# Two dense products of a float32 retention block by one level of Strassen

## The chip, the core and the metric

The kernel runs on one core of one Trainium2 chip. The metric is the device time in microseconds (us) of one execution. A profiled execution leaves a trace of every instruction; TensorE (PE) does matmuls, VectorE (DVE) and ScalarE (ACT) elementwise work, GpSimd (POOL) a little of it, and SyncE (SP) issues transfers. Weight loads of TensorE are listed as an engine of their own, PEld.

## What is computed

Two blocks in a row. The first is a recurrent retention layer (4 batches, 8 heads, 768 steps, head dimension 64), with a decay for each head:

```python
for t in range(S):
    state = gamma[None, :, None, None] * state + np.einsum('bhd,bhe->bhde', k[:, :, t], v[:, :, t])
    y[:, :, t] = scale * np.einsum('bhd,bhde->bhe', q[:, :, t], state)
```

Its result, laid out as x of 3072 tokens by 512, goes through two dense products with a leaky ReLU between:

```python
h = x @ w_in                      # 3072x512 @ 512x2048
g = np.maximum(0.01 * h, h)
return (g @ w_out).astype(np.float32)   # 3072x2048 @ 2048x512
```

Everything is computed in float32. The two weight matrices arrive as float64 and are rounded to float32 on the chip.

## The kernel before, in words

The 768 steps are cut into 6 chunks (`NC`) of 128 steps (`C`). A chunk has the same 128 steps of all 4 batches, so 512 tokens (`N`).

**Attention** of one batch of one chunk has three steps. `decay_v` lets POOL scale v by the decays (L86). `stage_a` makes the scores of the 8 heads on TensorE, even heads in one PSUM tile and odd heads in another (L97), and VectorE masks them (L102). `stage_y` multiplies the state by q (L116) and v by the masked scores (L121) into one PSUM tile `yp`; VectorE scales it into the token block `xt` (L124); then k times v (`sp`, L130) updates the state on VectorE (L134, L135). The score tiles, `yp` and `sp` share the PSUM tag `att` of 4 banks. The q/k and k/v data of a batch come in two transfers of 512 KB each on SP's queue (L80, L81), into three buffers, so three batches ahead.

**Weights** come in 32 pieces of 128 by 512 float64: 16 of `w_in`, then 16 of `w_out`. `round_words` turns a piece into float32 with five VectorE operations (L164, L169, L171, L173, L175) and two on ScalarE between the first and the fourth (L166, L167). Each rounding issues the load of the piece four further on. It all happens in the attention of chunk 0 (two pieces a batch) and in the dense products of chunk 0.

**Dense products.** `unit_h` makes 128 of the 2048 hidden features for the 512 tokens: 4 matmuls with the weights stationary and 512 token columns moving (L183), then ScalarE applies Prelu out of PSUM into `gt[f]` (L185). 16 such units make a chunk's hidden layer. `unit_o` makes the output of one batch with the hidden tokens stationary and 512 columns of `w_out` moving: 16 matmuls in four parts (L194); ScalarE copies the result (L198) and issues its store (L199).

**Order.** The order on every engine is written by hand: each engine runs its instructions in program order. The start runs the attention of chunk 0; then chunk by chunk 16 units of `unit_h` and 16 parts of `unit_o`, and in the gaps of these 32 steps the attention of the next chunk (`decay_v` at step 0 of 7 of a batch, `stage_a` at 1, `stage_y` at 4).

Of the kernel before, what the change touches and what calls it, by code (L numbers as in the profile page):

```python
# [20 lines left out]
def kernel(  # L21
# [22 lines left out]


    nc = tc.nc
    NC = S // C
    DM = H * D
    HP = H // 2
    KIN = DM // 128  # L50
    KOUT = DF // 128
    N = B * C
# [4 lines left out]
    work = ctx.enter_context(tc.tile_pool(name="work", bufs=2))  # L57
    psum = ctx.enter_context(
# [3 lines left out]
    dec = const.tile([128, HP * C + H + HP], FP32, name="dec")  # L62
    win = [[const.tile([128, W], FP32, name=f"win{r}_{i}") for i in range(KIN)]
           for r in range(DF // W)]
    wout = [const.tile([128, DM], FP32, name=f"wout{f}") for f in range(KOUT)]
    gt = [const.tile([128, N], FP32, name=f"gt{f}") for f in range(KOUT)]

# [6 lines left out]

    heads = {}

    def load(c, b):
        x = work.tile([128, 2, HP, C], FP32, tag="qk", bufs=3, name=f"qk_{c}_{b}")
        y = work.tile([128, 2, H, D], FP32, tag="kv", bufs=3, name=f"kv_{c}_{b}")
# [11 lines left out]
    def stage_a(c, b):  # L91
        x = heads[c, b][0]
        ps = [psum.tile([128, HP, C], FP32, tag="att", bufs=4, name=f"a{j}p_{c}_{b}")
              for j in range(2)]
        for a in range(HP):
            for j in range(2):
                nc.tensor.matmul(ps[j][:, a, :], lhsT=x[ts(j, 64), 1, a, :],  # L97
                                 rhs=x[ts(j, 64), 0, a, :])
        am = []
        for j in range(2):  # L100
            t = work.tile([128, HP, C], FP32, tag=f"am{j}", name=f"am{j}_{c}_{b}")
            nc.vector.tensor_tensor(out=t, in0=ps[j],  # L102
                                    in1=mask.unsqueeze(1).to_broadcast([128, HP, C]),
                                    op=ALU.mult)
            am.append(t)
        scores[c, b] = am

    def stage_y(c, b, xt):
        x, y = heads.pop((c, b))
        ks, vs = y[:, 0], y[:, 1]  # L110
        am = scores.pop((c, b))
        yp = psum.tile([128, HP, C], FP32, tag="att", bufs=4, name=f"yp_{c}_{b}")
        if c > 0:
            for a in range(HP):
                for j in range(2):
                    nc.tensor.matmul(yp[ts(j, 64), a, :], lhsT=st[b][ts(j, 64), a, :],  # L116
                                     rhs=x[ts(j, 64), 0, a, :], start=(a == 0), stop=False,
                                     skip_group_check=True)
        for a in range(HP):
            for j in range(2):  # L120
                nc.tensor.matmul(yp[ts(j, 64), a, :], lhsT=vs[:, 2 * a + j, :],  # L121
                                 rhs=am[j][:, a, :], start=(c == 0 and a == 0), stop=True,
                                 skip_group_check=True)
        nc.vector.tensor_tensor(out=xt[:, :, ts(b, C)], in0=yp, in1=gq, op=ALU.mult)  # L124
        if c == NC - 1:
            return
        sp = psum.tile([128, HP, D], FP32, tag="att", bufs=4, name=f"sp_{c}_{b}")
        for a in range(HP):
            for j in range(2):
                nc.tensor.matmul(sp[ts(j, 64), a, :], lhsT=ks[:, 2 * a + j, :],  # L130
                                 rhs=vs[:, 2 * a + j, :], start=(a == 0), stop=True,
                                 skip_group_check=True)
        if c > 0:
            nc.vector.tensor_tensor(out=st[b], in0=st[b], in1=sp, op=ALU.add)  # L134
        nc.vector.tensor_tensor(out=st[b], in0=st[b] if c > 0 else sp,  # L135
                                in1=gc.unsqueeze(2).to_broadcast([128, HP, D]), op=ALU.mult)


    pieces = [win[r][i] for r in range(DF // W) for i in range(KIN)] + wout
    first_out = KIN * (DF // W)  # L140
    raws = {}
    LOW, HIGH = 896 << 20, 1151 << 20

    def load_piece(n):
        if not f64:
            nc.sync.dma_start(out=pieces[n], in_=weights[n])
            return
        raws[n] = work.tile([128, W], I64, tag="raw", bufs=4, name=f"raw{n}")
        nc.sync.dma_start(out=raws[n], in_=weights[n])

    def round_piece(n):
        if f64:
            round_words(n)
        if n + 4 < len(pieces):
            load_piece(n + 4)

    def round_words(n):
        words = raws.pop(n).bitcast(U32).rearrange("p (n two) -> p n two", two=2)
        lo, hi = words[:, :, 0], words[:, :, 1]
        e = work.tile([128, W], U32, tag="e", name=f"e{n}")  # L160
        m = work.tile([128, W], U32, tag="m", name=f"m{n}")
        f = work.tile([128, W], FP32, tag="f", name=f"f{n}")

        nc.vector.tensor_scalar(out=e, in0=hi, scalar1=0x7FF00000, scalar2=None,  # L164
# [9 lines left out]
                                       op0=ALU.bitwise_and, op1=ALU.bitwise_or)  # L174
        nc.vector.scalar_tensor_tensor(out=pieces[n], in0=f, scalar=2.0 ** -20,  # L175
                                       in1=e.bitcast(FP32), op0=ALU.mult, op1=ALU.mult)


    def unit_h(c, f, xt):
        r, o = divmod(f * 128, W)  # L180
        hp = psum.tile([128, N], FP32, tag="h", name=f"hp_{c}_{f}")
        for i in range(KIN):
            nc.tensor.matmul(hp, lhsT=win[r][i][:, ds(o, 128)], rhs=xt[:, i, :],  # L183
                             start=(i == 0), stop=(i == KIN - 1))
        nc.scalar.activation(gt[f], hp, AF.Prelu, alpha=0.01)  # L185

    sums = {}

    def unit_o(c, b, part):
        if part == 0:  # L190
            sums[0] = psum.tile([128, DM], FP32, tag="o", name=f"op_{c}_{b}")
        op = sums[0]
        for f in range(4 * part, 4 * part + 4):
            nc.tensor.matmul(op, lhsT=gt[f][:, ts(b, C)], rhs=wout[f],  # L194
                             start=(f == 0), stop=(f == KOUT - 1))
        if part == KOUT // 4 - 1:
            ob = work.tile([128, DM], FP32, tag="ob", name=f"ob_{c}_{b}")
            nc.scalar.copy(out=ob, in_=op)  # L198
            nc.scalar.dma_start(out=out[ds(b * S + c * C, C), :], in_=ob)  # L199


    def new_xt(c):
        return work.tile([128, KIN, N], FP32, tag="xt", name=f"xt_{c}")

    def load_ahead(c, b):
        n = c * B + b + 3
        if n < NC * B:
            load(*divmod(n, B))

# [5 lines left out]
    load_piece(2)  # L215
    load_piece(3)
    load(0, 2)
# [4 lines left out]
    done = 0  # L222
    x = new_xt(0)
    for b in range(B):
        decay_v(0, b)
        stage_a(0, b)
        round_piece(done)
        round_piece(done + 1)
        done += 2
        stage_y(0, b, x)  # L230
        load_ahead(0, b)

    for c in range(NC):
        more = c + 1 < NC
        nx = new_xt(c + 1) if more else None
        for u in range(KOUT + 4 * B):
            if u < KOUT:
                unit_h(c, u, x)
            else:

                while done < min(len(pieces), first_out + 4 * (u - KOUT + 1)):
                    round_piece(done)
                    done += 1
                unit_o(c, *divmod(u - KOUT, KOUT // 4))
            if c == 0 and u < KOUT:
                round_piece(done)
                done += 1
            b, s = divmod(u, 7)
            if more and b < B:
                if s == 0:  # L250
                    decay_v(c + 1, b)
                elif s == 1:
                    stage_a(c + 1, b)
                elif s == 4:
                    stage_y(c + 1, b, nx)
                    load_ahead(c + 1, b)
        x = nx

# [19 lines left out]
def _layout(q, k, v, w_in, w_out):  # L278
# [10 lines left out]
    def tokens_first(x):  # L289
# [4 lines left out]
    DM, DF = w_in.shape  # L294
    w = np.concatenate([
        w_in.reshape(DM // 128, 128, DF // W, W).transpose(2, 0, 1, 3).reshape(-1, 128, W),
        w_out.reshape(DF // 128, 128, DM)])
    if w.dtype == np.float64:
# [28 lines left out]
```

## Time and profile before

| | us |
|---|---|
| median of 3 runs | 810.38 (809.5 to 811.61) |
| the profiled execution | 809.44 |
| its span, first to last instruction | 807.5 |

The page of the profile lists the busy time of each engine, the span in 40 slices, the chain of work that ended last, and groups of instructions by line. A row of a group reads: line, engine, operation, output<-input, partitions x elements, count | busy us, mean ns of one | idle time of the engine just before them, and who ended most of it. A row of the timeline reads: start in us, length in us, engine, line, operation, tiles, count. A float32 matmul leaves two records of matmul and two of weight load. The lengths of pipelined matmuls overlap, so a pitch is taken from start to start. Two facts to begin with: TensorE is busy for 768.1 us of the span, VectorE for 153.8, and most of VectorE's time is spent before 150 us, with the weights.

### The profile page before, as it was taken

What the parts mean: (1) busy time and instruction counts of PE and PEld (TensorE: products, weight loads), DVE (VectorE), ACT (ScalarE), POOL (GpSimd) and SP (SyncE); (2) the same over time, 40 slices, a digit from 0 to 9 for tenths busy, and PEclk for the clock granted to TensorE, in tenths of its full rate; (3) what the DMA queues carried; (4) which work ended last, traced back from release to release, by engine and by line L of the source; (5) the groups of instructions that cost most, each with busy time, mean ns of one, the idle gap of its engine ahead of it and who ended that gap; (6) DMA issues with size and microseconds to landing.
All of it is one profiled execution on the core that took longest, in us unless ns stands there. A gap on an engine that the chain in (4) does not pass through costs nothing.

```text
span 807.5 us, 6705 instructions
## 1 busy us (share of the span) xinstructions
PE 768.1 (95%) x2944; PEld 371.5 (46%) x2944; DVE 153.8 (19%) x269; ACT 111.4 (14%) x185; POOL 27.1 (3%) x29
## 2 busy tenths in 40 slices
PE   5489985999999999999999999999999999999998
PEld 4445432444454454545454444544444444444443
DVE  6968786100010010101010010100000000000000
ACT  2334342000111000111000111000111000111000
POOL 1100000000000000000000000000000000000000
PEclk8589996899999999999999999999999999999999
DMA  9645443020101210101201011102010000000000
GB/s 357 253 141 191 166 156 104 14 78 14 52 19 34 65 66 27 52 1 53 65 27 53 13 53 53 51 28 66 13 53 0 1 20 20 13 1 0 13 14 26
DMA packets 15148, 48.93 MB, mean 61 GB/s; under 512 B 1680, under 2 KB 1680, under 8 KB 15120
## 3 DMA queue, kind: packets, MB, share of 16 engines
q1 hardware_dynamic: 11664, 42.22, 15.3%
q10 hardware_dynamic: 3456, 6.29, 2.1%
q8 instruction: 23, 0.38, 0.2%
q14 instruction: 5, 0.04, 0.0%
HBM read 42.21 MB, written 6.29 MB: 60 GB/s over the span
## 4 chain that ended last, share of the span: by engine, by line
PE 90%; DVE 6%; ACT 2%; DMA 1%; issue 0%; SPq 0%
PE hp L183 42%; PE op L194 40%; PE yp L116 3%; PE yp L121 3%; PE a0p L97 2%; DVE e L173 1%; ACT e L167 1%; ACT e L166 1%; PE sp L130 1%; DVE wout L175 1%; DMA raw<-in_weights_dram 1%; DVE e L164 1%; DVE win L175 1%; DVE am L102 1%; DVE f L171 1%; DVE xt L124 0%
## 5 line engine op out<-in xcount | busy, mean ns | idle before, releaser
L194 PE MATMUL op<-wout,gt 128*128 128x512 f32 x768 | 342.9, 604 | 13.4 <-DVE wout L175 13.4
L183 PE MATMUL hp<-xt,win 128*128 128x512 f32 x768 | 337.8, 597 | 4.5 <-DVE xt L124 4.5
L194 PEld LDWEIGHTS op<-wout,gt 128*128 128x128 f32 x768 | 145.6, 192 | 195.4 <-issue 177.0
L183 PEld LDWEIGHTS hp<-xt,win 128*128 128x128 f32 x768 | 144.9, 191 | 181.5 <-issue 175.1
L185 ACT ACTIVATE gt<-hp 128x512 f32<-128x512 f32 x96 | 57.3, 597 | 298.2 <-PE hp L183 298.2
L102 DVE TENSOR_TENSOR am<-a0p,mask 128x512 f32<-128x512 f32 x24 | 16.5, 689 | 300.2 <-PE a1p L97 300.2
L198 ACT COPY ob<-op 128x512 f32<-128x512 f32 x24 | 14.0, 585 | 342.5 <-PE op L194 342.5
L124 DVE TENSOR_TENSOR xt<-yp,dec 128x512 f32<-128x512 f32 x24 | 16.6, 690 | 196.5 <-PE yp L121 196.5
L86 POOL TENSOR_TENSOR kv<-kv,dec 128x512 f32<-128x512 f32 x24 | 26.6, 1108 | 568.1 <-DMA kv<-in_kv_dram 563.0
L121 PE MATMUL yp<-am,kv 128*64 128x128 f32 x384 | 31.6, 304 | 13.7 <-issue 12.5
L97 PEld LDWEIGHTS a0p<-qk 64*128 64x128 f32 x192 | 25.4, 203 | 19.8 <-issue 14.6
L97 PE MATMUL a0p<-qk 64*128 64x128 f32 x192 | 30.2, 302 | 4.3 <-DMA qk<-in_qk_dram 4.3
L121 PEld LDWEIGHTS yp<-am,kv 128*64 128x64 f32 x384 | 24.4, 150 | 19.0 <-issue 16.5
L97 PE MATMUL a1p<-qk 64*128 64x128 f32 x192 | 30.2, 302 | 0.0
L166 ACT ACTIVATE e<-e 128x512 uint32<-128x512 uint32 x32 | 20.1, 627 | 50.6 <-DVE e L164 50.5
L173 DVE SCALAR_TENSOR_TENSOR e<-raw,e 128x512 uint32<-128x512 uint32 x32 | 22.6, 705 | 19.6 <-ACT e L167 19.6
L97 PEld LDWEIGHTS a1p<-qk 64*128 64x128 f32 x192 | 25.4, 203 | 0.0
L116 PEld LDWEIGHTS yp<-qk,st 64*64 64x64 f32 x320 | 17.7, 137 | 15.9 <-issue 15.2
L171 DVE SCALAR_TENSOR_TENSOR f<-raw,m 128x512 f32<-128x512 uint32 x32 | 23.8, 743 | 1.1
L116 PE MATMUL yp<-qk,st 64*64 64x128 f32 x320 | 22.6, 282 | 0.0
L167 ACT ACTIVATE e<-e 128x512 uint32<-128x512 uint32 x32 | 20.2, 630 | 1.0
L102 DVE TENSOR_TENSOR am<-a1p,mask 128x512 f32<-128x512 f32 x24 | 16.3, 681 | 0.0
(16 smaller groups left out, 101.5 us busy)
## 6 DMA issues: line engine op xcount, KB each, us to landing
raw<-in_weights_dram SPq DMA_DIRECT2D x32, 512.0 KB, 3.4
qk<-in_qk_dram SPq DMA_DIRECT2D x24, 512.0 KB, 3.4
kv<-in_kv_dram SPq DMA_DIRECT2D x24, 512.0 KB, 4.4
out_dram<-ob ACTq DMA_DIRECT2D x24, 256.0 KB, 2.0
dec<-decay_dram SPq DMA_DIRECT2D x1, 262.0 KB, 4.6
```

The lines of the kernel that those rows point to most:

```text
L86: nc.gpsimd.tensor_tensor(out=v, in0=v, in1=gk.unsqueeze(2).to_broadcast([128, H, D]), op=ALU.mult)
L97: nc.tensor.matmul(ps[j][:, a, :], lhsT=x[ts(j, 64), 1, a, :], rhs=x[ts(j, 64), 0, a, :])
L102: nc.vector.tensor_tensor(out=t, in0=ps[j], in1=mask.unsqueeze(1).to_broadcast([128, HP, C]), op=ALU.mult)
L116: nc.tensor.matmul(yp[ts(j, 64), a, :], lhsT=st[b][ts(j, 64), a, :], rhs=x[ts(j, 64), 0, a, :], start=(a == 0), stop=False, skip_group_che ...
L121: nc.tensor.matmul(yp[ts(j, 64), a, :], lhsT=vs[:, 2 * a + j, :], rhs=am[j][:, a, :], start=(c == 0 and a == 0), stop=True, skip_group_che ...
L166: nc.scalar.activation(e, e, AF.Relu, scale=-1.0, bias=float(HIGH))
L167: nc.scalar.activation(e, e, AF.Relu, scale=-8.0, bias=8.0 * (HIGH - LOW))
L171: nc.vector.scalar_tensor_tensor(out=f, in0=lo, scalar=2.0 ** -32, in1=m, op0=ALU.mult, op1=ALU.add)
L173: nc.vector.scalar_tensor_tensor(out=e, in0=hi, scalar=0x80000000, in1=e, op0=ALU.bitwise_and, op1=ALU.bitwise_or)
L183: nc.tensor.matmul(hp, lhsT=win[r][i][:, ds(o, 128)], rhs=xt[:, i, :], start=(i == 0), stop=(i == KIN - 1))
L185: nc.scalar.activation(gt[f], hp, AF.Prelu, alpha=0.01)
L194: nc.tensor.matmul(op, lhsT=gt[f][:, ts(b, C)], rhs=wout[f], start=(f == 0), stop=(f == KOUT - 1))
```

## The change

Both dense products are made by one level of Strassen's scheme in the form with few additions: a product of matrices cut into 2 by 2 blocks takes 7 block products instead of 8, and sums of blocks before and after.

- **Blocks.** A chunk's 512 tokens become two halves of 256 (two batches each), the 512 input dimensions two halves of 256, and the hidden features are taken in 4 units of 512, two halves of 256 each. The token block `x` holds four blocks of 256 tokens by 256 dimensions; `t` holds three differences of them. VectorE makes these with four operations a chunk (`differences`), the fourth in place.
- **Weights.** `win[u]` and `wout[u]` hold, for each of 4 units, four blocks and three sums; `sums` makes the sums with four VectorE operations once a unit is rounded. The pieces come in the order win 0, 1, wout 0, 1, win 2, 3, wout 2, 3.
- **Products.** `seven` runs the products M1, M6, M5, M4, M2, M7, M3, weights stationary, 256 token columns moving. A unit of the hidden layer has 4 matmuls a product, a half of the output (`output`, two units at once) 8. Four PSUM banks (A to D) serve the seven: M2 is added onto M1 in bank A, M7 onto M6 in B, M3 onto M5 in C. M1 and M6, M5 are read out of their bank before.
- **After the products.** `hidden` makes five additions on VectorE, two copies and four Prelu on ScalarE, and the four differences of its result for the second product. `output` does likewise; its first half leaves sums in `o`, the second adds to them and stores the four blocks, on SP's queue.
- **PSUM and SBUF.** The dense products have 6 banks, the attention tag `att` 2 instead of 4. q/k and k/v have two buffers for three, the raw weights three for four, the rest of the work tiles mostly one.
- **Order.** In the start one piece a batch is rounded; in chunk 0 four pieces in each hidden unit; after the first two hidden units the whole attention of chunk 1 with four pieces; eight pieces in the first output half. In later chunks the attention of one batch of the next chunk stands in each hidden unit.
- The output leaves in another layout and is transposed on the host.

The core of the diff:

```diff
-        ps = [psum.tile([128, HP, C], FP32, tag="att", bufs=4, name=f"a{j}p_{c}_{b}")
+        ps = [psum.tile([128, HP, C], FP32, tag="att", bufs=2, name=f"a{j}p_{c}_{b}")
...
+    units = [win[0], win[1], wout[0], wout[1], win[2], win[3], wout[2], wout[3]]
+    pieces = [w[:, 2 * h : 2 * h + 2, i, :] for w in units for h in range(2) for i in range(2)]
...
-        if n + 4 < len(pieces):
-            load_piece(n + 4)
+        if n + 3 < len(pieces):
+            load_piece(n + 3)
+        if n % 4 == 3:
+            sums(units[n // 4])
...
+    def sums(w):
+        plus(w[:, 4], w[:, 1], w[:, 3])
+        minus(w[:, 1], w[:, 0], w[:, 1])
+        minus(w[:, 5], w[:, 4], w[:, 0])
+        minus(w[:, 6], w[:, 2], w[:, 5])
+
+    def differences(x, t):
+        minus(t[:, 0], x[:, 1], x[:, 0])
+        minus(t[:, 1], x[:, 3], t[:, 0])
+        minus(t[:, 2], x[:, 2], t[:, 1])
+        minus(x[:, 1], x[:, 3], x[:, 1])
...
+        which = [("M1", "A", 0, 0), ("M6", "B", 5, 5), ("M5", "C", 4, 4), ("M4", "D", 3, 6),
+                 ("M2", "A", 2, 2), ("M7", "B", 1, 1), ("M3", "C", 6, 3)]
+        for m, bank, sa, sb in which:
+            first = bank not in banks
+            if first:
+                banks[bank] = psum.tile([128, 2, N], FP32, tag="ff", bufs=6, name=f"{bank}_{name}")
+            ps = banks[bank]
+            for i in range(2):
+                for n, (w, x, t) in enumerate(tiles):
+                    rhs = x[:, sb] if sb < 4 else t[:, sb - 4]
+                    for k in range(2):
+                        nc.tensor.matmul(
+                            ps[:, i, :], lhsT=w[:, sa, k, ts(i, 128)], rhs=rhs[:, k, :],
+                            start=(first and i == 0 and n == 0 and k == 0),
+                            stop=(n == len(tiles) - 1 and k == 1), skip_group_check=True)
+            takes(m, ps)
+            yield
...
+            if m == "M1":
+                got["m1"] = temp("m1", at)
+                nc.scalar.copy(out=got["m1"], in_=ps)
+            elif m == "M6":
+                got["u2"] = temp("u2", at)
+                plus(got["u2"], got["m1"], ps)
+            elif m == "M5":
+                got["m5"] = temp("m5", at)
+                nc.scalar.copy(out=got["m5"], in_=ps)
+            elif m == "M4":
+                got["m4"] = ps
+            elif m == "M2":
+                nc.scalar.activation(g[:, 0], ps, AF.Prelu, alpha=0.01)
+            elif m == "M7":
+                got["u3"] = temp("u3", at)
+                plus(got["u3"], got["m1"], ps)
+                plus(g[:, 3], got["u3"], got["m5"])
+                leaky(3)
+                plus(g[:, 2], got["u3"], got["m4"])
+                leaky(2)
+            elif m == "M3":
+                plus(g[:, 1], got["u2"], ps)
+                leaky(1)
+                differences(g, gd)
...
+        for p in range(NU // 2):
...
+                for step, _ in enumerate(hidden(c, u, x, t, g, gd)):
+                    if c == 0 and step in (1, 3, 4, 6):
+                        round_piece()
+                    if c > 0:
+                        early(step - 1, u)
+            if c == 0 and p == 0:
+                for b in range(B):
+                    early(0, b)
+                    round_piece()
+                    early(3, b)
+            for step, _ in enumerate(output(c, p, o, parts)):
+                if c == 0 and p == 0:
+                    round_piece()
+                    if step == 6:
+                        round_piece()
+                if p == 1 and step == 1 and more:
+                    nt = new_t(c + 1)
+                    differences(nx, nt)
```

More of the change, by code (lines that the diff above doesn't have):

```diff
@@ L62 @@
     dec = const.tile([128, HP * C + H + HP], FP32, name="dec")
[L63 to L66, printed above, removed]
+    win = [const.tile([128, 7, 2, 256], FP32, name=f"win{u}") for u in range(NU)]
+    wout = [const.tile([128, 7, 2, 256], FP32, name=f"wout{u}") for u in range(NU)]
     st = [const.tile([128, HP, D], FP32, name=f"st{b}") for b in range(B)]
@@ L123, in stage_y @@
                                  skip_group_check=True)
[L124 to L140, printed above, removed]
+        th, o = divmod(b * C, N)
+        blocks = xb.rearrange("p (kh th) k n -> p kh th k n", th=2)[:, :, th, :, ds(o, C)]
+        nc.vector.tensor_tensor(out=blocks, in0=yp.rearrange("p (kh k) t -> p kh k t", k=2),
+                                in1=gq.rearrange("p (kh k) t -> p kh k t", k=2), op=ALU.mult)
+        if c < NC - 1:
+            sp = psum.tile([128, HP, D], FP32, tag="att", bufs=2, name=f"sp_{c}_{b}")
+            for a in range(HP):
+                for j in range(2):
+                    nc.tensor.matmul(sp[ts(j, 64), a, :], lhsT=ks[:, 2 * a + j, :],
+                                     rhs=vs[:, 2 * a + j, :], start=(a == 0), stop=True,
+                                     skip_group_check=True)
+            if c > 0:
+                nc.vector.tensor_tensor(out=st[b], in0=st[b], in1=sp, op=ALU.add)
+            nc.vector.tensor_tensor(out=st[b], in0=st[b] if c > 0 else sp,
+                                    in1=gc.unsqueeze(2).to_broadcast([128, HP, D]), op=ALU.mult)
+        n = c * B + b + AHEAD
+        if n < NC * B:
+            load(*divmod(n, B))
+    units = [win[0], win[1], wout[0], wout[1], win[2], win[3], wout[2], wout[3]]
+    pieces = [w[:, 2 * h : 2 * h + 2, i, :] for w in units for h in range(2) for i in range(2)]
     raws = {}
+    done = [0]
     LOW, HIGH = 896 << 20, 1151 << 20
@@ L174, in round_words @@
                                        op0=ALU.bitwise_and, op1=ALU.bitwise_or)
[L175 to L199, printed above, removed]
@@ L202, in new_xt, with plus @@
[L202 to L208, printed above, removed]
+        nc.vector.scalar_tensor_tensor(
+            out=pieces[n], in0=f.rearrange("p (h n) -> p h n", h=2), scalar=2.0 ** -20,
+            in1=e.bitcast(FP32).rearrange("p (h n) -> p h n", h=2), op0=ALU.mult, op1=ALU.mult)
+    def plus(out, a, b):
+        nc.vector.tensor_tensor(out=out, in0=a, in1=b, op=ALU.add)
@@ new lines, in temp, with hidden, leaky, takes @@
+    def temp(name, at):
+        return work.tile([128, 2, N], FP32, tag=name, name=f"{name}_{at}")
+    def hidden(c, u, x, t, g, gd):
+        got = {}
+        at = f"{c}_{u}"
+        def leaky(i):
+            nc.scalar.activation(g[:, i], g[:, i], AF.Prelu, alpha=0.01)
+        def takes(m, ps):
+            if m == "M1":
[22 more added lines that the diff above has]
+                differences(g, gd)
+        return seven([(win[u], x, t)], f"h{at}", takes)
@@ new lines, in output, with store, takes @@
+    def output(c, p, o, parts):
+        got = {}
+        at = f"{c}_{p}"
+        def store(i):
+            if p == 1:
+                nc.sync.dma_start(out=out[c, i], in_=o[:, i])
+        def takes(m, ps):
+            if m == "M1":
+                got["m1"] = temp("m1", at)
+                nc.scalar.copy(out=got["m1"], in_=ps)
+            elif m == "M6":
+                got["u2"] = temp("u2", at)
+                plus(got["u2"], got["m1"], ps)
+                if p == 1:
+                    plus(o[:, 1], got["u2"], o[:, 1])
+            elif m == "M5":
+                got["m5"] = temp("m5", at)
+                if p == 0:
+                    nc.scalar.copy(out=got["m5"], in_=ps)
+                else:
+                    plus(got["m5"], o[:, 3], ps)
+            elif m == "M4":
+                if p == 0:
+                    nc.scalar.copy(out=o[:, 2], in_=ps)
+                else:
+                    plus(o[:, 2], o[:, 2], ps)
+            elif m == "M2":
+                if p == 0:
+                    nc.scalar.copy(out=o[:, 0], in_=ps)
+                else:
+                    plus(o[:, 0], o[:, 0], ps)
+                store(0)
+            elif m == "M7":
+                got["u3"] = temp("u3", at)
+                plus(got["u3"], got["m1"], ps)
+                plus(o[:, 3], got["u3"], got["m5"])
+                store(3)
+                plus(o[:, 2], got["u3"], o[:, 2])
+                store(2)
+            elif m == "M3":
+                plus(o[:, 1], got["u2"] if p == 0 else o[:, 1], ps)
+                store(1)
+        tiles = [(wout[2 * p + i], *parts[i]) for i in range(2)]
+        return seven(tiles, f"o{at}", takes)
@@ L210, with new_x, new_t @@
+    def new_x(c):
+        return work.tile([128, 4, 2, N], FP32, tag="x", bufs=2, name=f"x_{c}")
+    def new_t(c):
+        return work.tile([128, 3, 2, N], FP32, tag="t", name=f"t_{c}")
     load(0, 0)
@@ L220 @@
                             base=0, pattern=[[1, 128]], channel_multiplier=-1)
-    done = 0
-    x = new_xt(0)
+    x = new_x(0)
     for b in range(B):
@@ L226 @@
         stage_a(0, b)
-        round_piece(done)
-        round_piece(done + 1)
-        done += 2
+        round_piece()
         stage_y(0, b, x)
-        load_ahead(0, b)
+    t = new_t(0)
+    differences(x, t)
     for c in range(NC):
         more = c + 1 < NC
[L235 to L256, printed above, removed]
@@ L257, with early @@
-        x = nx
+        o = work.tile([128, 4, 2, N], FP32, tag="o", name=f"o_{c}")
+        nx = new_x(c + 1) if more else None
+        def early(step, b):
+            if not more:
+                return
+            if step == 0:
+                decay_v(c + 1, b)
+                stage_a(c + 1, b)
+            elif step == 3:
+                stage_y(c + 1, b, nx)
+        for p in range(NU // 2):
+            parts = []
+            for i in range(2):
+                u = 2 * p + i
+                g = work.tile([128, 4, 2, N], FP32, tag=f"g{i}", name=f"g_{c}_{u}")
+                gd = work.tile([128, 3, 2, N], FP32, tag=f"gd{i}", name=f"gd_{c}_{u}")
+                parts.append((g, gd))
+                for step, _ in enumerate(hidden(c, u, x, t, g, gd)):
+                    if c == 0 and step in (1, 3, 4, 6):
+                        round_piece()
+                    if c > 0:
+                        early(step - 1, u)
[8 more added lines that the diff above has]
+                    if step == 6:
+                        round_piece()
+                if p == 1 and step == 1 and more:
+                    nt = new_t(c + 1)
+                    differences(nx, nt)
@@ L260 @@
+        if more:
+            x, t = nx, nt
 _OUT = (3072, 512)
```

59 lines of the change are left out of this document (38 added, 21 removed).

## The prediction

> **What bounds the kernel now.** I read the page first (busy shares, slices, chain), then the busy time by stage, then the chain in order of time, then the timeline of single stretches.
>
> ```profile
> span 807.5 us, 6705 instructions
> PE 768.1 (95%) x2944; PEld 371.5 (46%) x2944; DVE 153.8 (19%) x269; ACT 111.4 (14%) x185; POOL 27.1 (3%) x29
> PEclk8589996899999999999999999999999999999999
> PE 90%; DVE 6%; ACT 2%; DMA 1%; issue 0%; SPq 0%
> ```
>
> TensorE holds 90% of the chain that ended last. But the shares are a mean over two different regimes, which the table by stage parts (columns: stretch, its length, then busy time and count of PE, PEld, DVE, ACT, POOL, granted clock, DMA share, GB/s):
>
> ```profile
> 0.00:42.56 42.56, 20.11 (x192) 17.80 (x192) 34.07 (x57) 11.37 (x17) 7.71 (x11) 0.72 0.76 293
> 42.56:192.48 149.92, 136.55 (x513) 63.83 (x514) 79.01 (x141) 39.98 (x67) 5.84 (x5) 0.92 0.33 113
> 192.48:318.33 125.85, 125.85 (x513) 60.94 (x513) 10.93 (x20) 11.89 (x20) 4.17 (x4) 1.00 0.13 42
> 570.03:694.02 123.99, 123.99 (x449) 58.66 (x449) 7.92 (x12) 11.89 (x20) 1.04 (x1) 1.00 0.05 17
> 694.02:803.92 109.90, 109.87 (x256) 48.36 (x255) 0.00 (x0) 11.89 (x20) 0.00 (x0) 1.00 0.03 10
> 803.92:807.50 3.58, 0.00 (x0) 0.00 (x0) 0.00 (x0) 0.58 (x1) 0.00 (x0) 0.98 0.19 73
> ```
>
> So: a start of 42.56 us on VectorE (34 of it busy); chunk 0 until 192.48, still mixed with the rounding of the weights; chunks 1 to 5 in which TensorE never stops; a tail of 3.58 us. Chunks 1 to 4 take 694.02 - 192.48 = 501.54 us.
>
> ```profile
> 694.02 54.93 PE hp L183 x128
> 748.95 54.95 PE op L194 x128
> ```
>
> Chunk 5 is dense products alone: 256 matmul records (each float32 matmul leaves two) in 109.88 us, 429.2 ns a record of 512 columns.
>
> **The steady chunks.** Before, a chunk has 256 records of 512 columns. After: 4 units of 7 products of 4 matmuls, and 2 output halves of 7 products of 8 matmuls, 112 + 112 = 224 matmuls, 448 records of 256 columns. Halving the columns doubles the weight loads for the same stream, so the question is the pitch of a 256-column record. No row has it; the nearest are 512 columns above and the 128-column score matmuls:
>
> ```profile
> 325.12 0.37 PE L97 MATMUL a0p<-qk 64*128 64x128 f32 x1
> ...
> 325.34 0.27 PE L97 MATMUL a0p<-qk 64*128 64x128 f32 x1
> 325.34 0.19 PEld L97 LDWEIGHTS a0p<-qk 64*128 64x128 f32 x1
> 325.45 0.27 PE L97 MATMUL a0p<-qk 64*128 64x128 f32 x1
> ...
> 326.01 0.27 PE L97 MATMUL a0p<-qk 64*128 64x128 f32 x1
> ...
> 326.32 0.69 DVE L102 TENSOR_TENSOR am<-a0p,mask 128x512 f32<-128x512 f32 x1 [27.73 <-PE a1p L97]
> ```
>
> Six steps from 325.34 to 326.01: 111.7 ns for 128 columns, with 128 weight columns loaded for each. The load is recorded at 190 ns, begins with the matmul before, and yet the next matmul starts 110 ns later: the recorded length isn't serial. A straight line between 111.7 ns at 128 and 429.2 ns at 512 gives 217.5 ns at 256, which I take. Ends: 214.6 (half of 512) and 223.4 (twice the 128).
>
> The Trainium skill, page "TensorE: Matmul & The Clock Gate", section "Back-to-back issue gap", speaks against this: in a stream of load and matmul pairs it gives about 81 ns at 128 columns where the stream alone is 56, so short matmuls pay for their loads. As an estimate from that page, 25 ns on each of 2688 records would be 67 us, and the kernel would be slower. The rows above disagree, with 111.7 ns against a quarter of 429.2, which is 107.3: 4 ns, not 25.
>
> Per chunk: 448 x 0.2175 = 97.4 us for 256 x 0.4292 = 109.9: 12.5 saved. The attention of the next chunk stays as it is: 125.85 - 109.9 = 16 us a chunk, drains included. Chunks 1 to 4: 501.54 - 4 x 12.5 = 451.5. Chunk 5: 97.4.
>
> ```profile
> L185 ACT ACTIVATE gt<-hp 128x512 f32<-128x512 f32 x96 | 57.3, 597 | 298.2 <-PE hp L183 298.2
> ...
> raw<-in_weights_dram SPq DMA_DIRECT2D x32, 512.0 KB, 3.4
> qk<-in_qk_dram SPq DMA_DIRECT2D x24, 512.0 KB, 3.4
> kv<-in_kv_dram SPq DMA_DIRECT2D x24, 512.0 KB, 4.4
> ```
>
> What has to hide beside it: 36 additions of the hidden units, 14 of the output, 4 token differences, at the 0.65 us that I take below, 35 us, with the 10.9 us of attention 46 of 113 us: VectorE has room. The tightest wait in a steady chunk is the output's second product, which needs the second token difference of the unit just ended: after M3 come one addition, Prelu on ScalarE (0.60), two differences, some 3.4 us with VectorE's backlog; the output's M1 (16 records, 3.5 us) and the first half row of M6 (0.9) cover it with 1 us to spare. If that cover went, 11 outputs would pay the lack. M2, M7 and M3 add into banks read three to four products (5 us and more) earlier, by one operation. Six banks for four a unit: each bank asked for was read in the unit before.
>
> **Chunk 0, where it is paid for.** Here VectorE sets the pace. Its prices:
>
> ```profile
> L124 DVE TENSOR_TENSOR xt<-yp,dec 128x512 f32<-128x512 f32 x24 | 16.6, 690 | 196.5 <-PE yp L121 196.5
> L135 DVE TENSOR_TENSOR st<-st,dec 128x256 f32<-128x256 f32 x16 | 6.8, 425 | 0.6
> ```
> ```profile
> 113.69 0.69 DVE L173 SCALAR_TENSOR_TENSOR e<-raw,e 128x512 uint32<-128x512 uint32 x1 [0.29 <-ACT e L167]
> ...
> 114.42 0.69 DVE L175 SCALAR_TENSOR_TENSOR wout<-f,e 128x512 f32<-128x512 f32 x1
> ...
> 116.80 0.69 DVE L173 SCALAR_TENSOR_TENSOR e<-raw,e 128x512 uint32<-128x512 uint32 x1 [0.30 <-ACT e L167]
> ```
> ```profile
> 61.47 0.69 DVE L173 SCALAR_TENSOR_TENSOR e<-raw,e 128x512 uint32<-128x512 uint32 x1 [0.62 <-ACT e L167]
> ...
> 64.91 0.69 DVE L173 SCALAR_TENSOR_TENSOR e<-raw,e 128x512 uint32<-128x512 uint32 x1 [0.61 <-ACT e L167]
> ```
> ```profile
> 134.50 1.09 POOL L86 TENSOR_TENSOR kv<-kv,dec 128x512 f32<-128x512 f32 x1 [33.10 <-DMA kv<-in_kv_dram]
> 134.72 1.41 DVE L171 SCALAR_TENSOR_TENSOR f<-raw,m 128x512 f32<-128x512 uint32 x1
> ```
>
> A 512-element operation follows the one that it depends on by 0.73 us, others by 0.60: 0.65 as a mean, so 2.6 for four (the sums of one weight unit, or the differences of one token block). One weight piece: 3.1 us alone, 3.4 when Prelu shares ScalarE; I take 3.3. While POOL scales a v, one VectorE operation lasts 1.41 for 0.69: 0.75 more.
>
> ```profile
> 4.26 0.58 PE L97 MATMUL a0p<-qk 64*128 64x128 f32 x1 [4.26 <-DMA qk<-in_qk_dram]
> ...
> 6.44 0.69 DVE L102 TENSOR_TENSOR am<-a0p,mask 128x512 f32<-128x512 f32 x1 [5.38 <-PE a1p L97]
> ```
> ```profile
> 33.94 0.68 DVE L102 TENSOR_TENSOR am<-a0p,mask 128x512 f32<-128x512 f32 x1
> ```
> ```profile
> 42.56 8.91 PE hp L183 x16
> 192.48 6.87 PE hp L183 x16
> ```
>
> Start. Three batches before take 33.94 - 6.44 = 27.5, 9.2 each with two pieces. After: one piece (-3.1), but with two attention banks for four the next scores can't start until xt and st have read theirs, so VectorE waits for a round of score matmuls: 6.44 - 4.26 = 2.2 at the low clock (at full clock 325.12 to 326.32, 1.2). 8.3 a batch; batch 3's scores are masked from 31.3. Then mask 1.2, piece 3.3, sums 2.6, xt 0.6: the first product can start at 39, the differences end at 42.3. M1 and M6 are 3.5 us, plus 2 for the clock (8.91 against 6.87): VectorE's first addition at **44.5**.
>
> Unit 0: additions u2, u3, g3, g2, g1 (3.4), the Prelu awaited (0.7), differences 2.6, four pieces 13.2, sums 2.6: 22.5 us of VectorE for 28 x 2 x 0.2175 = 12.2 of TensorE: until 67. Unit 1: M6 needs the sums just made and VectorE then waits for it (1.7 to 3.4, taken 2.5), plus 22.5: **92**. Attention of chunk 1: 4 x (mask 1.2, piece 3.3, POOL 0.75, xt 0.6, st twice 0.8) + 3 waits of 2.3 + sums 2.6: 36, **128**. Output half 0: eight pieces 26.4, two sums 5.2, five additions 3.3: 35 for 24.4 of TensorE, **163**. Units 2 and 3, whose weights are now ahead: 22.5 each, **208**. Output half 1: M1 and a quarter of M6 are done by then; 5.75 products of 3.48 are 20 us: chunk 0 ends at **228**, 35.5 later than before.
>
> Ends: with pieces at 3.1, score waits at 1.2 and no wait for M6, 6 + 7 + 2.5: 212. With every wait for TensorE at the low clock and VectorE held up by a copy ahead of it in ScalarE's queue, 20 more: 248. DMAs stay covered: pieces three ahead for four have 6.6 us against 3.4 to land; heads two ahead for three have a batch of 8 against 4.4. Stores move from ACT's queue to SP's, behind loads that wait for matmuls already past. The tail keeps its form: one operation, one store, 3.6.
>
> **Sum.** 228 + 451.5 + 97.4 + 3.6 = 780.5 of span; the profiled run took 809.44 for a span of 807.5, so 1.9 around it: **782 us**, against 809.44 (and a median of 810.38): 27 less, 3.4%. Pitch: -7 to +14 over some 2460 records outside VectorE's stretches; chunk 0: -16 to +20.
>
> **The rivals.**
>
> ```profile
> 671.18 1.02 PE yp L116 x16
> 672.20 1.02 PE yp L121 x16
> ```
>
> (a) Slower: the weight load sets the pitch. For it: here two 64-column loads and two 128-column matmuls take 1.02 / 8 = 127.5 ns where L97 takes 111.7; something in loading costs 16 ns. On 2688 records that is 43 us: 825. It decides from 10 ns a record (27 / 2688). Against: these change the tile form, the dense products don't, and L97 loads full columns. The page's rule above is this rival, at a higher price.
>
> (b) Slower: a wait in place of work. If a reader of one part of a tile waits for writes to all of it, the output's M1 waits for the last difference: addition 0.7, Prelu 0.6 and two hand-overs of 0.1, differences 2.6, less the 0.9 that the first unit covers, some 3.5 on 11 outputs, 39 us: 821. The trace of before has no tile that is read in one part while another is due to be written, so it neither shows nor excludes it.
>
> (c) No gain: the saving comes, but chunk 0 eats all of it.
>
> ```profile
> 49.88 0.69 DVE L173 SCALAR_TENSOR_TENSOR e<-raw,e 128x512 uint32<-128x512 uint32 x1 [5.65 <-ACT e L167]
> ```
>
> Before, rounding once waited 5.65 us because its ScalarE steps stood behind a Prelu that waited for TensorE. After, 24 pieces stand behind such copies; 1.1 us more on each gives chunk 0 at 255 and 809. Against: TensorE is ahead of VectorE in all but the first two units.
>
> **Chances.** Forecast 0.82, its own range 766 to 800; (a) 0.05, (b) 0.07, (c) 0.06. A measurement of this kernel tells 0.3% from no change. (c) spreads around 809: 0.02 of it faster, 0.03 same, 0.01 slower. Together faster 0.84, same 0.03, slower 0.13. The range, 766 to 806, takes in the bounds of the forecast's terms and the lower part of (c).
>
> **What would show it.** The 256-column pitch in a steady chunk at 215 to 223 ns (233: rival a); TensorE without idle time in chunks 1 to 5, above all ahead of the output's M1 and M6 (rival b); a chunk of 113 us; VectorE nearly always busy until 208 and chunk 1 beginning near 228, with idle time of VectorE put down to score matmuls and M6, little to ScalarE (rival c). I am wrong if chunk 1 begins after 255 or a steady chunk takes over 118.

## The result and the profile after

| | before | after |
|---|---|---|
| median, us | 811.0 (4 runs) | 769.85 (4 runs) |
| ratio to before, 95% interval | 1 | 0.949 (0.946 to 0.953) |
| profiled execution, us | 809.44 | 768.5 |
| its span, us | 807.5 | 766.2 |

The kernel is 5.1% faster; 782 was predicted, within 766 to 806. First the page of the changed kernel: span, engines, granted clock, and the chain that ended last by engine.

```profile
span 766.2 us, 9520 instructions
PE 697.3 (91%) x4096; PEld 600.1 (78%) x4096; DVE 387.6 (51%) x625; ACT 144.0 (19%) x239; POOL 27.0 (4%) x29
PEclk9997799888899999999999999999999999999999
PE 77%; DVE 15%; ACT 6%; issue 1%; DMA 1%; DVEq 0%
```

VectorE's busy time has gone from 153.8 to 387.6 us, and its share of the chain from 6% to 15%. Whether that hurts depends on the stage. The table by stage (length, then busy time and count of PE, PEld, DVE, ACT, POOL, granted clock, DMA share, GB/s), cut at the first dense product and at the ends of the chunks:

```profile
0.00:33.19 33.19, 22.58 (x193) 19.81 (x193) 19.55 (x34) 6.33 (x9) 6.02 (x10) 1.00 0.71 261
33.19:216.68 183.49, 129.13 (x706) 108.14 (x706) 150.04 (x253) 51.15 (x85) 6.37 (x5) 0.86 0.31 107
216.68:329.36 112.68, 112.68 (x706) 97.42 (x705) 47.53 (x74) 17.31 (x29) 4.17 (x4) 1.00 0.15 47
554.71:665.53 110.82, 110.82 (x642) 95.14 (x641) 43.62 (x66) 17.31 (x29) 2.08 (x2) 1.00 0.09 29
665.53:762.24 96.71, 96.70 (x449) 84.77 (x447) 33.04 (x50) 17.31 (x29) 0.00 (x0) 1.00 0.03 11
762.24:766.20 3.96, 0.00 (x0) 0.00 (x0) 0.69 (x1) 0.00 (x0) 0.00 (x0) 0.81 0.24 88
```

From chunk 1 on TensorE is busy all the time, as before, but for 112.7 us a chunk instead of 125.85, and 96.7 in the last instead of 109.9. Chunk 0 ends at 216.68 instead of 192.48: it pays 24 us back. Beside the terms of the prediction:

| term, us | predicted | measured |
|---|---|---|
| end of chunk 0 | 228 | 216.7 |
| chunks 1 to 4 | 451.5 | 448.85 |
| chunk 5 | 97.4 | 96.7 |
| tail | 3.6 | 4.0 |
| span | 780.5 | 766.2 |

Of the 14.3 us between forecast and result, 11.3 lie in chunk 0. Its stretches are found in the timeline by VectorE's operations. Two products on which TensorE waits for it, the first as the chain has it and as the timeline has it:

```profile
62.34 3.80 PE B_h L236 x8
```
```profile
62.34 3.78 PE L236 MATMUL B_h<-t,win 128*128 128x256 f32 x8 [10.95 <-DVE win L205]
```
```profile
195.08 4.34 PE L236 MATMUL B_o<-gd,wout 128*128 128x256 f32 x12 [10.95 <-DVE wout L205]
```

Both are an M6 (bank B). Before each, TensorE stands still for 10.95 us until the third sum of a weight unit is made: from 33.19 on, VectorE is busy for 150.0 us of chunk 0 and TensorE for 129.1, so the stream of products is shorter than VectorE's work for it, as the prediction had it.

### The profile page after: what moved, and what is told of

It is laid out like the page before. It is cut to its first block, busy times and chain, and to the rows that moved or that the text cites. A ratio compares the mean times of both kernels' runs of the same rounds, so it can differ in the third digit from the quotient of the medians.

```text
span 766.2 us, 9520 instructions
## 1 busy us (share of the span) xinstructions
PE 697.3 (91%) x4096; PEld 600.1 (78%) x4096; DVE 387.6 (51%) x625; ACT 144.0 (19%) x239; POOL 27.0 (4%) x29
## 4 chain that ended last, share of the span: by engine, by line
PE 77%; DVE 15%; ACT 6%; issue 1%; DMA 1%; DVEq 0%
PE B_h L236 10%; PE B_o L236 10%; PE C_o L236 10%; PE A_o L236 9%; PE C_h L236 9%; PE A_h L236 9%; PE D_o L236 5%; PE D_h L236 5%; PE a0p L107 3%; DVE e L195 3%; ACT e L188 3%; ACT e L189 3%; PE yp L126 2%; PE yp L131 2%; DVE wout L197 2%; DVE win L197 1%
## 5 line engine op out<-in xcount | busy, mean ns | idle before, releaser
L236 PE MATMUL A_h<-x,win 128*128 128x256 f32 x384 | 94.6, 391 | 9.7 <-ACT m L256 9.7
L236 PEld LDWEIGHTS A_h<-x,win 128*128 128x128 f32 x384 | 74.9, 196 | 21.2 <-ACT m L256 10.5
L236 PE MATMUL A_o<-g,wout 128*128 128x256 f32 x384 | 87.4, 380 | 0.5 <-DVE wout L197 0.3
L236 PEld LDWEIGHTS A_o<-g,wout 128*128 128x128 f32 x384 | 72.7, 190 | 11.2 <-ACT g L266 0.7
L236 PE MATMUL B_h<-t,win 128*128 128x256 f32 x192 | 47.4, 391 | 14.3 <-DVE win L205 11.0
L236 PE MATMUL B_o<-gd,wout 128*128 128x256 f32 x192 | 45.1, 389 | 10.9 <-DVE wout L205 10.9
L236 PEld LDWEIGHTS B_o<-gd,wout 128*128 128x128 f32 x192 | 37.5, 196 | 16.7 <-DVE wout L205 11.3
L236 PE MATMUL B_h<-x,win 128*128 128x256 f32 x192 | 49.0, 400 | 1.7 <-DVE u L202 1.7
L236 PE MATMUL C_h<-t,win 128*128 128x256 f32 x192 | 48.3, 395 | 0.0
L236 PE MATMUL C_h<-x,win 128*128 128x256 f32 x192 | 45.8, 382 | 0.1
L236 PE MATMUL D_h<-t,win 128*128 128x256 f32 x192 | 45.4, 379 | 0.0
```

Of the source, the lines that this page charges most:

```text
L236: nc.tensor.matmul(ps[:, i, :], lhsT=w[:, sa, k, ts(i, 128)], rhs=rhs[:, k, :], start=(first and i == 0 and n == 0 and k == 0), stop=(n == ...
```

## The experiments

Each kernel differs from the changed one (or, where it says so, from the one before) by the edit shown.

### Eight products instead of seven

```diff
-        which = [("M1", "A", 0, 0), ("M6", "B", 5, 5), ("M5", "C", 4, 4), ("M4", "D", 3, 6),
-                 ("M2", "A", 2, 2), ("M7", "B", 1, 1), ("M3", "C", 6, 3)]
+        for fh, th in ((0, 0), (0, 1), (1, 0), (1, 1)):
+            # one bank: w[2*kh + fh] times x[2*kh + th], kh = 0, 1
...
-            sums(units[n // 4])
...
-    differences(x, t)
```

> The same blocks, banks, order and 256-token columns, but eight block products added up in PSUM, and no sums, differences or additions. If the gain of the steady chunks is the eighth product alone, a steady chunk takes 512 records x 0.2158 us + 15.5 us of attention = 126 us instead of 112.2, and the last one 110.5; chunk 0, without some 53 us of VectorE work, ends near 172 instead of 217; together 172 + 504 + 110.5 + 4 = 790, 792 us in all. If the gain came from the new arrangement (weights stationary, other order), steady chunks stay near 112 and the time goes below 730.

Measured: 794.56 us, ratio 0.980 (0.977 to 0.982). Table by stage, chunk 0, chunk 1 and one half of chunk 5:

```profile
0.00:171.09 171.09, 150.24 (x961) 131.63 (x962) 111.18 (x200) 51.94 (x85) 11.69 (x15) 0.94 0.46 166
171.09:297.57 126.48, 126.48 (x769) 109.57 (x769) 13.68 (x24) 11.90 (x20) 4.17 (x4) 1.00 0.12 42
```
```profile
730.44 27.63 PE E_h L333 x128
758.07 27.64 PE E_o L333 x128
```

A steady chunk takes 126.5 us. The 13.8 us by which the changed kernel lies below it are the eighth product (64 records of 215.8 ns); the arrangement alone brings nothing there, 126.48 us for 125.85. 128 records take 27.63 us: 215.9 ns each, as with seven products. But chunk 0 ends at 171.1, 21 us before that of the old kernel. So the change is two changes. The new arrangement (two halves of the tokens, pieces of both matrices in turns, weights stationary) is worth 18 us of span, 807.5 to 789.5. Strassen on top of it is worth another 23, 789.5 to 766.2 (by the medians 16 and 25): it saves 13.8 in each of five chunks, 69 in all, and costs 45.6 in chunk 0, where VectorE has 58 us less to do without it (111.2 us for 169.6).

### The columns cut in two, in the old kernel

```diff
-            nc.tensor.matmul(hp, lhsT=win[r][i][:, ds(o, 128)], rhs=xt[:, i, :],
-                             start=(i == 0), stop=(i == KIN - 1))
+            for s in range(2):
+                nc.tensor.matmul(hp[:, ts(s, N // 2)], lhsT=win[r][i][:, ds(o, 128)],
+                                 rhs=xt[:, i, ts(s, N // 2)], start=(i == 0 and s == 0),
+                                 stop=(i == KIN - 1), skip_group_check=True)
```

and the same for the output's matmuls.

> The kernel before with every dense matmul cut into two of 256 columns, each with its own weight load; the products are the same. If a load hides behind 256 columns, 3072 records of 215.8 ns take 663 us for 659, so the time goes up by 3 to 4 us, to 813 or 814. If each load costs 16 ns (rival a of the prediction), it goes up by 49, to 860.

Measured: 813.24 us, ratio 1.003 (1.002 to 1.005). Its chain in chunk 5, where twice as many records stand as before:

```profile
696.93 55.25 PE hp L184 x256
752.18 55.27 PE op L197 x256
```

256 records in 55.25 us, 215.8 ns; 110.52 for the chunk instead of 109.88. Twice the weight loads cost 0.64 us a chunk. Rival (a), the load as the bound, falls, in a kernel that has nothing else of the change.

### The three sums out of PSUM

```diff
-                 ("M2", "A", 2, 2), ("M7", "B", 1, 1), ("M3", "C", 6, 3)]
+                 ("M2", "E", 2, 2), ("M7", "F", 1, 1), ("M3", "G", 6, 3)]
...
-                nc.scalar.activation(g[:, 0], ps, AF.Prelu, alpha=0.01)
+                plus(g[:, 0], got["m1"], ps)
+                leaky(0)
...
-                plus(g[:, 1], got["u2"], ps)
+                plus(got["m5"], got["m5"], ps)
+                plus(g[:, 1], got["u2"], got["m5"])
```

and likewise in `output`.

> The seven products each in a bank of their own, the three sums that were added up in PSUM made on VectorE instead: two operations more for each set of seven, some of them taken over from ScalarE. If VectorE sets the pace in chunk 0 alone, ten of these (0.65 us each) lengthen chunk 0 by 6 to 7 us, to 223, and a steady chunk stays at 112.2: 776 us. If VectorE's work also sets the pace of the steady chunks, 12 operations a chunk add 7.8 us in each: 815.

Measured: 778.4 us, ratio 0.960 (0.958 to 0.963). Chunk 0 and two chunks behind it:

```profile
0.00:222.36 222.36, 148.70 (x897) 125.92 (x898) 175.78 (x297) 57.64 (x94) 12.47 (x15) 0.88 0.35 128
222.36:335.04 112.68, 112.68 (x706) 97.42 (x705) 55.33 (x86) 17.35 (x29) 5.21 (x4) 1.00 0.14 47
335.04:449.00 113.96, 113.33 (x706) 97.35 (x706) 55.84 (x87) 17.35 (x29) 5.13 (x4) 1.00 0.13 47
```

Chunk 0 grows by 5.7 us. Chunk 1 has 8 us more of VectorE's work than in the changed kernel (55.33 to 47.53) and is exactly as long. The one after ends at 448.88, a little before its row does, and so takes 113.8. It is not quite dense (113.33 of 113.96): in one of its output halves M6 waits 0.51 us for a difference. The addition that is new behind M3 eats the reserve ahead of the output's M6, to which an experiment below returns. So adding up in PSUM is worth some 9 us in all, most of it in chunk 0.

### Chunk 0 by eight products, the sums later

```diff
+                if c == 0:
+                    for step, _ in enumerate(hidden8(c, u, x, g)):
+                        round_piece()
...
+                        if step in (3, 4, 5, 6):
+                            sums(win[step - 3])
+                        if step in (5, 6):
+                            sums(wout[step - 5])
...
+                if c == 1 and p == 0:
+                    sums(wout[2 + i])
```

Four sums of `w_in` and two of `w_out` are asked for in the last output half of chunk 0, the other two in chunk 1, and the attention of chunk 1 is spread over the products of chunk 0. From chunk 1 on all else is as in the changed kernel.

> Chunk 0 by eight products added up in PSUM, with the weights in the order of the changed kernel; the sums of the weights are made in the last output half of chunk 0 and in chunk 1, from chunk 1 on all is as in the changed kernel. The attention of chunk 1 is spread over the matmuls of chunk 0. If what is left of chunk 0 is VectorE's sums, differences and additions, chunk 0 becomes bound by TensorE (start 37, 110.5 of products, 16 of attention) and ends near 166: 166 + 449 + 97 + 4 = 716, 718 us in all. If the sums only move the wait into chunk 1 (21 us on VectorE beside its 46 a chunk), chunk 1 grows by 10 or more: 728. If chunk 0 is held by the rounding of the weights itself, it ends near 190: 742.

Measured: 716.75 us, ratio 0.883 (0.880 to 0.886). One of its four executions took 4099 us, for a cause that isn't known; the median contains it, the ratio does not. Four more of the same kernel, under the name late2, took 714 to 717.

> The same kernel as before with chunk 0 by eight products and the sums made later, once more: 717 us, within 3.

Measured: 715.6 us, ratio 0.882 (0.880 to 0.884). From the profile of the first set of executions (in that of late2 chunk 0 ends at 163.57): chunk 0, chunk 1 with half of the late sums in it, and chunk 2:

```profile
0.00:164.65 164.65, 148.98 (x961) 128.07 (x962) 123.45 (x217) 51.47 (x85) 12.40 (x15) 0.97 0.48 171
164.65:277.32 112.67, 112.67 (x705) 97.41 (x705) 59.44 (x94) 17.30 (x29) 4.17 (x4) 1.00 0.14 49
277.32:390.00 112.68, 112.68 (x706) 97.42 (x705) 46.95 (x74) 17.30 (x29) 4.17 (x4) 1.00 0.14 47
```

Chunk 0 becomes 52 us shorter, and chunk 1, with 12.5 us more on VectorE than chunk 2, no longer: 112.67. So the sums of the weights cost nothing here, where TensorE sets the pace. In chunk 0 VectorE is spared the additions and differences of seven products and half of the sums, 46 us of work in all (123.5 us for 169.6), and TensorE, with one seventh more products than in the changed kernel, is done far sooner. The eight products account for 45.6 of the 52 us, by the first experiment, which makes no sums at all; the other 6 go with the spread attention, which was not tried by itself.

### Four banks and four

```diff
-        ps = [psum.tile([128, HP, C], FP32, tag="att", bufs=2, name=f"a{j}p_{c}_{b}")
+        ps = [psum.tile([128, HP, C], FP32, tag="att", bufs=4, name=f"a{j}p_{c}_{b}")
...
-                banks[bank] = psum.tile([128, 2, N], FP32, tag="ff", bufs=6, name=f"{bank}_{name}")
+                banks[bank] = psum.tile([128, 2, N], FP32, tag="ff", bufs=4, name=f"{bank}_{name}")
```

> The changed kernel with four PSUM banks for the products instead of six, and four for the attention instead of two. VectorE waited 15.7 us for score matmuls in all, 5.8 of it before the first; with four banks the scores of the next batch are made while VectorE still works, so up to 9 us of VectorE's stretch in chunk 0 go: chunk 0 ends near 208, 761 us. A steady chunk stays at 112.7, if each bank asked for has been read in time also with four. If the products need their six banks, a steady chunk grows and the time stays at 770 or above.

Measured: 765.17 us, ratio 0.943 (0.942 to 0.945); chunk 0 ends at 213.3, and a steady chunk is again 112.68. The waits of VectorE up to the last weight sum (us in total, times, longest), in the changed kernel:

```profile
DVE am L112 <- PE a0p L107: 7.2, 6, 1.8
DVE am L112 <- PE a1p L107: 5.8, 1, 5.8
DVE u L202 <- PE B_h L236: 4.0, 2, 3.2
```

and with four and four:

```profile
DVE am L112 <- PE a1p L107: 7.0, 3, 5.6
DVE u L202 <- PE B_h L236: 4.9, 2, 3.3
DVE am L112 <- PE a0p L107: 1.0, 1, 1.0
```

Behind the first scores, 7.2 us of waiting become 2.4, one new microsecond stands at M6, and the chunk is 3.4 shorter. The expected 9, and so 761 us, were too much: they had counted waits of later chunks, where they cost nothing, and of the 4.8 us of waiting that go in chunk 0 not all shows in its length. The products of this kernel don't need six banks.

### The reserve ahead of the output's second product

```diff
                 leaky(1)
+                for again in range(2):
+                    minus(gd[:, 0], g[:, 1], g[:, 0])
+                    minus(gd[:, 1], g[:, 3], gd[:, 0])
                 differences(g, gd)
```

> The first two differences of each hidden unit are made three times over, the same values each time: four operations more, about 2.7 us, between the Prelu and the difference that the output's second product needs. In the trace of the changed kernel that difference is done some 0.8 us before its first reader. If that wait is the tightest of a steady chunk, TensorE then waits 1.9 us in each of ten output halves of chunks 1 to 5, and chunk 0 grows by four times 2.7: 770 + 19 + 11 = 800, a steady chunk 116.5. If VectorE's order doesn't matter in a steady chunk, only chunk 0 grows: 781.

Measured: 804.25 us, ratio 0.992 (0.990 to 0.993). Chunk 1, and one output half in the timeline:

```profile
228.97:345.94 116.97, 113.20 (x706) 97.39 (x705) 57.80 (x90) 17.30 (x29) 4.17 (x4) 1.00 0.13 46
```
```profile
262.83 0.69 DVE L205 TENSOR_TENSOR gd<-g 128x512 f32<-128x512 f32 x1 [0.70 <-ACT g L251]
...
264.43 1.03 PE L236 MATMUL B_o<-gd,wout 128*128 128x256 f32 x4
...
266.45 1.42 DVE L205 TENSOR_TENSOR gd<-g,gd 128x512 f32<-128x512 f32 x2
267.20 2.86 PE L236 MATMUL B_o<-gd,wout 128*128 128x256 f32 x12 [1.75 <-DVE gd L205]
```

The first four records of M6 belong to the unit before last and run; the next twelve wait 1.75 us for the difference that ends at 267.1. Chunk 0 is 12.3 us longer, for 10.8 expected. A steady chunk is 4.3 us longer: 2.9 us of extra work on an engine that is busy for less than half of the chunk costs about 2 us each time it is asked for at this place. In the experiment with the three sums out of PSUM, 8 us at other places cost nothing in chunk 1.

### Both together

Chunk 0 by eight products, and four banks and four.

> Chunk 0 by eight products with the sums made later, and four banks for the products and four for the attention. With chunk 0 bound by TensorE the banks act on the start alone, where VectorE waits for score matmuls (some 5 us of the first 32): 711 to 713 us. If the attention is not what holds the start, 717 as with six and two.

Measured: 714.17 us, ratio 0.881 (0.879 to 0.882). Its executions (713.8 to 715.5) overlap with those of six and two (713.8 to 717.5, without the one of 4099), so a gain of the banks is not clear here. The trace shows what they do: the first product starts at 27.8 instead of 31 to 32, and the first of chunk 1 at 160.1 instead of 163.4 to 164.5. Then about half of the gain is lost.

```profile
160.07 1.89 PE L234 MATMUL A_h<-x,win 128*128 128x256 f32 x8
```
```profile
168.71 1.99 PE L234 MATMUL D_h<-t,win 128*128 128x256 f32 x8 [2.01 <-DVE o L200]
```

M4 of chunk 1 waits 2.01 us for an addition of chunk 0's last output half, which reads a bank and stands on VectorE behind the late sums. So with the late sums four banks are once too few; this wait is more than what is missing to the expected 711 to 713. The kernel beats both others: 11.9% below the one before, 7% below the changed one.

## Why the prediction was right, and where its sizes were off

**The steady chunks: right.** The pitch at 256 columns was taken at 217.5 ns, from a straight line between two rows, and is 215.8. The lower row differs in form too, which the working passes over: its score matmuls are 64 rows high, and in the 111.7 ns two of them run side by side (a0p and a1p start within 0.01 us of each other). That it still led to the right pitch was in part luck; the columns cut in two are the proper test.

The Trainium skill gives a formula for an isolated matmul (page "TensorE: Matmul & The Clock Gate", section "Back-to-back issue gap": columns over 2.4 GHz plus 2.5 ns). As an estimate from that page, with two streams a record, which is chosen to fit and which no run here shows by itself, it is 215.8 at 256 and 429.2 at 512; the traces have these values. The same section's 81 ns for a stream of load and matmul pairs is for 128 columns, and no run here has dense products of 128. At 256 float32 columns such a cost of the load isn't seen: in the kernel with cut columns 256 more records a chunk cost 0.64 us, 2.5 ns each.

**What hides beside them: right.** VectorE was put at 46 of 113 us and is at 47. The wait named as the tightest, the output's M6, is the tightest: it was given 1 us to spare, the changed kernel shows 0.8, and the repeated differences show the price beyond it.

```profile
251.55 1.42 DVE L205 TENSOR_TENSOR gd<-g,gd 128x512 f32<-128x512 f32 x2
252.14 3.62 PE L236 MATMUL B_o<-gd,wout 128*128 128x256 f32 x16
```

The first of these two operations, some 0.7 us, is the difference in question, done near 252.25; its first reader is the fifth record of M6, 0.86 us behind 252.14: a reserve of some 0.8.

**Chunk 0: right in kind, 11.3 us too long.** By VectorE's milestones (predicted, measured): first addition 44.5 and 41.1; sums after unit 0 67 and 63.0; after unit 1 92 and 88.0; attention of chunk 1 128 and 118.1; output half 0 163 and 152.1; units 2 and 3 208 and 195.7; end 228 and 216.7. By stretch that is 3.4 us less in the start, 5.9 in the attention of chunk 1 and 3.0 in unit 0, output half 0 and units 2 and 3 together, and 1.0 more in output half 1; unit 1 came out even. Three terms were mis-sized.

One is the term "3 waits of 2.3" for the scores, with two attention banks for four.

```profile
94.65 0.69 DVE L112 TENSOR_TENSOR am<-a0p,mask 128x512 f32<-128x512 f32 x1 [0.58 <-PE a0p L107]
```

The wait is 0.58 us, not 2.3. The working let the scores begin when xt *and* st had read their banks. In the trace the scores start at 93.33, right behind the start of the first state operation, and VectorE's two state operations (0.8, until 94.06) run while TensorE already fills the first bank. Three such waits are 5 us of the 6 by which that stretch was too long. In the start the wait is 1.8 for 2.2; a pair of score matmuls takes 0.21 us there and 0.11 at 94 us, although the granted clock is recorded as 1.00 in both.

Another is the piece at 3.3 us, a mean of 3.1 and 3.4. Nearly all take 3.1, as these two do:

```profile
68.61 0.69 DVE L195 SCALAR_TENSOR_TENSOR e<-raw,e 128x512 uint32<-128x512 uint32 x1 [0.30 <-ACT e L189]
...
71.73 0.69 DVE L195 SCALAR_TENSOR_TENSOR e<-raw,e 128x512 uint32<-128x512 uint32 x1 [0.30 <-ACT e L189]
```

0.2 on 28 pieces is 5.6 us; in unit 1 a longer wait for M6, 3.2 us for the 2.5 taken, makes up for it. The longer pitch came from stretches of the old kernel in which a Prelu stood in ScalarE's queue ahead of the rounding every 3.4 us, and VectorE waited 0.61 us for ScalarE in each piece; here it waits 0.3 in every one.

The third is the start. It was given 8.3 us a batch, and the batches took 7.2 to 7.9. It was given M1 and M6, with 2 us for a low clock, behind the last tokens; but M1 had run before, and M6, alone from 39.03 on, took 1.8.

**The rivals.** (a), the load as the bound, is ruled out by the kernel with cut columns. (b) (its terms add up to 3.2 us, not 3.5, so 817 for 821), a reader of one part that waits for writes to the whole tile, is ruled out by the trace: M1 of unit 0 runs while the rest of its token block is still to be written.

```profile
33.19 2.51 PE L236 MATMUL A_h<-x,win 128*128 128x256 f32 x8
...
36.65 0.68 DVE L136 TENSOR_TENSOR x<-yp,dec 128x512 f32<-128x512 f32 x1
```

That is also why the first product ran at 33 and not at 39: it reads two batches' tokens. M6 then waited for the differences until 39.03, so what the early start gained is not clear. (c), chunk 0 eats all of the gain because rounding waits for ScalarE, did not happen: these waits are 9.5 us over all 32 pieces, 0.3 at the longest. Chunk 0 does eat much, 45.6 of Strassen's 69 us, but by VectorE's own work, and the arrangement brings 21 there.

**What the prediction didn't see.** It worked out chunk 0 as a whole and so had the arrangement's gain in its sum without knowing it. Of the 21 us, 11 lie ahead of the first product (at 42.56 before, at 31.26 with eight products, where one piece a batch is rounded and not two), 10 behind it. In the old kernel the first output of chunk 0 needs all 16 pieces of `w_out`, and the table of waits shows TensorE idle for 13.4 us on them; in the new order half of them do for an output half, and in the trace of the eight products no such wait is left. That this is the cause of the 10 us was not tried by itself.

## What to carry to other kernels

Price an algorithm that trades matmuls for additions stage by stage. Where TensorE sets the pace, a saved product is saved in full and additions on an engine that is half idle are free, except at the one place where the next product waits for them; where the other engine sets the pace, additions lengthen the stage nearly in full, and here the plain algorithm is the faster one. The best kernel here uses both: eight products in the first chunk, seven in the others, with the sums of the weights made late, where VectorE has room for them.

## What was not expected

A float32 matmul of full 128 by 128 weights pays almost nothing for its weight load down to 256 columns: 429.2 ns a record at 512, 215.8 at 256, with a weight load recorded at some 190 ns in each. And the extra products of a plain chunk 0 were so much cheaper than the additions, differences and sums that they replaced: 14 us more of TensorE's stream, 46 us less of chunk.
